# RWKV-5 recurrence and a hierarchical mixture of experts: three items computed in blocks of 32 tokens, small items first, a ring of four weight buffers

## The chip, the cores and the metric

The kernel runs on one core of one Trainium2 chip. The metric is device time in microseconds; of a kernel's runs the median counts. A core has TensorE (PE in the profile; PEld is its weight load), VectorE (DVE), ScalarE (ACT), GpSimd (POOL) and SyncE (SP). SP only issues DMAs here. The profile is of one execution, with times from the start of its span.

## The reference

Two blocks follow each other. The first is a linear recurrence over 768 steps for 4 batches of 8 heads of width 48. Its output is read as 3072 tokens of width 384. The second sends each token to one of 4 groups and to one of 4 experts of that group, and runs that expert alone:

```python
for t in range(S):
    cur = np.einsum('bhd,bhe->bhde', u[None] * kt, vt)
    y[:, :, t] = np.einsum('bhd,bhde->bhe', rt, state + cur)
    state = w[None, :, :, None] * state + np.einsum('bhd,bhe->bhde', kt, vt)
...
for g in range(G):
    ...
    for e in range(Eg):
        mask_e = e_idx == e
        h = np.maximum(xg[mask_e] @ w1[g, e], 0.0)
        ye = h @ w2[g, e]
        combined = g_w[mask_g][mask_e] * e_w[mask_e]
        out[tok_idx] = combined[:, None] * ye
```

All is FP32. w1 of an expert is 384 x 1024, w2 is 1024 x 384, 3.15 MB together, and there are 16 experts.

## The kernel before

**First stage, up to about 137 us.** The recurrence is computed in chunks of 128 steps. While it runs, tokens are routed and their rows (384 values, a token number and a gate, in four quarters of 98 values) are scattered by POOL to `x_sorted` in HBM, to a region for each expert. When most tokens are routed, the two experts with the most tokens so far are chosen. Their weights are fetched early (`early[0]`, `early[1]`, two pairs of buffers), and their first 128 tokens each are computed ahead (`up_ahead`, `down_ahead`, L1042 to L1061).

Of this stage only one group of instructions matters later: `gate_parts` (L646) writes four matmuls with 32 output rows each to the partition quarters 0, 32, 64 and 96 of one PSUM tile. The array has 128 columns, and each of these uses a group of 32.

**Second stage: the items.** The 16 experts are then worked off as items. `order` (L1073) is the list of slots 1, 2, ..., 15, 0. `SLOTS` gives the number of tokens that a slot computes. Slots 0 and 1 are what is left of the two early experts (96 and 88 tokens), slots 2 to 15 are the other experts, the largest first (212 down to 164). An item at place p has these steps:

- `fetch_rows(p)` (L1093): SP fetches its tokens' rows into `xg`, four DMAs, one for each quarter. Rows have 392 bytes. For the slots 0 and 1 a fifth DMA (L1110) fetches token numbers and gates.
- `fetch_weights(p)` (L1112): SP fetches w1 and w2 in eight DMAs of 384 KB each (L136, L142).
- `columns(p)` (L1119): DVE turns the rows into columns, `xe` (L1123), and makes the list of output rows.
- `arrange(p)` (L1135): ACT copies w2 into another order, `w2p`, in three copies (L1141).
- `up` (L1143), four calls for an item: TensorE multiplies w1, the stationary side, with `xe`, whose columns are tokens. ACT applies Relu into `hT`.
- `down` (L1158), three calls: TensorE multiplies `w2p`, stationary, with `hT`; ACT copies the result to `yT`.
- `finish(p)` (L1168): DVE turns `yT` back (L1172), multiplies by the gates (L1173), and POOL scatters each block of 32 tokens to the output (L1175).

Slots 0 and 1 go another way down: `rows_down` (L239) and `half_down` (L253) have `hT` stationary and w2 streaming in 384 or 2 x 192 columns, ACT scales by the gate (L245, L260), and POOL scatters whole or half rows (L246, L261).

There are three pairs of weight buffers in turn, `turns` (early[1] and two more), and early[0] is kept until the last item. SP works in program order. Its order is: three pieces of weights of p=1, rows 0, rows 1, the other pieces, rows 2, weights 2, and then in item p the rows of p+2 (from p=1 on) and the weights of p+3. Written out: weights 1 (with rows 0 and 1 among them), rows 2, weights 2, weights 3, rows 3, weights 4, rows 4, weights 5 and so on. The DMAs of SP signal over eight semaphores in turn; one is issued when the DMA that had its semaphore last has landed.

Of the kernel before, what the change touches and what calls it, by code (L numbers as in the profile page):

```python
# [21 lines left out]
SLOTS = [96, 88, 212, 208, 208, 202, 202, 200, 200, 196, 194, 188, 186, 174, 172, 164]  # L22
# [7 lines left out]
def kernel(  # L30
# [36 lines left out]
    assert len(SLOTS) == GE and max(SLOTS) <= 256 and sorted(SLOTS[2:], reverse=True) == SLOTS[2:]  # L67

# [50 lines left out]
    tagA = [cst([P, 2], f"tagA_{i}") for i in range(4)]  # L119
    idA = [cst([P, 1], f"idA_{i}", I32) for i in range(4)]  # L120
    idH = [cst([P, 1], f"idH_{z}", I32) for z in range(2)]
    okA = [cst([P, 1], f"okA_{i}", I32) for i in range(4)]
# [130 lines left out]
    def half_down(hT, w2, i, n, z, po, yt):  # L253
        cols = slice(DM // 2 * z, DM // 2 * (z + 1))
        for fo in range(FO):
            nc.tensor.matmul(
                po[0:n, 0 : DM // 2], lhsT=hT[:, fo, 0:n], rhs=w2[:, fo, cols], start=(fo == 0), stop=(fo == FO - 1),
                skip_group_check=True,
            )
        nc.scalar.mul(yt[0:n], po[0:n, 0 : DM // 2], tagA[i][0:n, 1:2])  # L260
        ins = nc.gpsimd.indirect_dma_start(  # L261
            out=out.rearrange("n (z w) -> (n z) w", z=2),
            out_offset=bass.IndirectOffsetOnAxis(ap=idH[z][0:n].bitcast(U32), axis=0),
            in_=yt[0:n], in_offset=None, bounds_check=2 * N - 1, oob_is_err=False,
        )
        tc.declare_no_dep(ins.ins, group="rows out", reason="no piece comes twice")
        tc.add_to_no_dep_group("rows out", ins.ins)

    def tokens(i, n, count, halves=False):
        tag = tagA[i][0:n, 0:1].bitcast(I32)  # L270
        nc.vector.tensor_scalar(out=okA[i][0:n], in0=prow[0:n], scalar1=count[0:n], scalar2=None, op0=OP.is_lt)
        if halves:
            for z in range(2):
                nc.vector.memset(idH[z][0:n], NOWHERE)
            nc.vector.tensor_scalar(out=tag, in0=tag, scalar1=1, scalar2=None, op0=OP.logical_shift_right)
            nc.vector.copy_predicated(idH[0][0:n], okA[i][0:n], tag)
            nc.vector.tensor_scalar(out=tag, in0=tag, scalar1=1, scalar2=None, op0=OP.bitwise_or)
            nc.vector.copy_predicated(idH[1][0:n], okA[i][0:n], tag)
            return
# [783 lines left out]
    with ExitStack() as moe:  # L1063
# [9 lines left out]
        order = list(range(1, GE)) + [0]  # L1073
        last = GE - 1
        turns = [early[1]] + [
# [7 lines left out]
        def held(p):  # L1083
            return early[0] if p == last else turns[p % 3]
# [8 lines left out]
        def fetch_rows(p):  # L1093
# [15 lines left out]
            if s < 2:  # L1109
                nc.sync.dma_start(out=tagA[2 + s][0 : SLOTS[s]], in_=mine[0 : SLOTS[s], Q_ID : Q_ID + 2])  # L1110

# [7 lines left out]
        def columns(p):  # L1119
# [4 lines left out]
            if s < 2:  # L1124
                tokens(2 + s, SLOTS[s], cnt_s[:, s : s + 1], p == last)
                return
# [41 lines left out]
        def finish(p):  # L1168
# [5 lines left out]
            for i in range(nb):  # L1174
                ins = nc.gpsimd.indirect_dma_start(  # L1175
                    out=out_q, out_offset=bass.IndirectOffsetOnAxis(ap=idn[:, i : i + 1].bitcast(U32), axis=0),
                    in_=yt[:, i], in_offset=None, bounds_check=N * NQ - 1, oob_is_err=False,
                )
                tc.declare_no_dep(ins.ins, group="rows out", reason="no piece comes twice")
                tc.add_to_no_dep_group("rows out", ins.ins)  # L1180

        fetch_weights(1, range(3))
        fetch_rows(0)
        fetch_rows(1)
        fetch_weights(1, range(3, NPIECE))
        fetch_rows(2)
        fetch_weights(2)
        columns(0)
# [302 lines left out]
```

## Time and profile before

| | |
|---|---|
| median of 14 runs | 420.35 us (413.02 to 423.34) |
| profiled execution | 414.87 us |
| its span | 413.1 us |
| mean granted TensorE clock | 0.983 |
| item p=0 (slot 1) begins | 161.03 us |
| item p=15 (slot 0) begins | 394.32 us |
| its first and second down half begin | 399.65 and 402.25 us |
| last scatter on POOL | 407.44 us, 0.92 us long |

The profile's page gives the busy time of each engine, then the same in slices, then groups of instructions. The timeline gives instructions in order of time, equal ones merged: start, length from the first to the end of the last, engine, line, operation, tiles, shape, count, and in brackets the idle time before and what ended it. The list of waits gives who waited for what, in total, how often, and the longest. The bracket of a wait names what came last by the profile, and can be off where that had long been done. Ends of matmuls are modelled, their starts are recorded.

The weights' last set of pieces is issued between 354.1 and 363.2 us. The rows' DMA on SP (L1105) is issued, for p=2, at 164.89 us, for p=3 at 189.43, for p=4 at 205.63.

### The profile page before, as it was taken

The page shows a single profiled execution, that of the slowest core. Times are in us where ns is not written, and L with a number is a line of the kernel's source. Part 1 is how long each engine was busy: PE and PEld are TensorE (multiplying, and loading weights), DVE is VectorE, ACT ScalarE, POOL GpSimd, SP SyncE. Part 2 cuts the span into 40 slices and gives each one's busy share as a digit, 9 for nine tenths or more (in the row PEclk, how much of TensorE's full clock was granted, in tenths as well). Part 3 has the DMA queues.
Part 4 walks back from the last instruction along what each step waited for, and adds up shares of the span by engine and source line. Part 5 has one row for each costly group of instructions (what it writes and reads, how often), then busy time and mean ns, then how long its engine had stood idle before and what let it go on. Part 6 is the DMA issues. An engine that isn't in the chain of part 4 may idle for free.

```text
span 413.1 us, 10511 instructions
## 1 busy us (share of the span) xinstructions
PE 395.3 (96%) x3989; PEld 367.5 (89%) x3989; DVE 154.1 (37%) x408; ACT 180.0 (44%) x429; POOL 202.5 (49%) x266
## 2 busy tenths in 40 slices
PE   8999999999879899999999999999999999998992
PEld 6788998888768777799999999999999999998991
DVE  7888988878638431101112112021221221121110
ACT  4666888888545211414424324144143244243210
POOL 7999979987410242001461441623624523532542
PEclk9999999999969899999999999999999999999998
DMA  9999999978939256999999999899989889891000
GB/s 135 177 173 187 213 203 208 223 153 199 297 87 263 87 175 166 274 263 250 238 255 264 212 229 278 208 246 263 214 237 272 217 235 272 197 243 35 27 21 23
DMA packets 121198, 81.80 MB, mean 198 GB/s; under 512 B 94902, under 2 KB 112370, under 8 KB 121141
## 3 DMA queue, kind: packets, MB, share of 16 engines
q1 hardware_dynamic: 114083, 71.12, 75.1%
q0 software_dynamic: 4768, 9.55, 8.0%
q10 hardware_dynamic: 2290, 0.40, 0.7%
q8 instruction: 33, 0.54, 0.6%
q14 instruction: 24, 0.20, 0.2%
HBM read 69.89 MB, written 11.67 MB: 197 GB/s over the span
## 4 chain that ended last, share of the span: by engine, by line
issue 45%; PE 32%; POOL 18%; DVE 2%; another core or an unknown queue 1%; POOLq 1%; ACT 0%; DVEq 0%
POOL out_dram L1175 16%; PE PA L564 6%; PE YB L611 6%; PE TR L545 3%; PE YB L602 2%; PE RW L545 2%; PE TR L646 2%; PE YB L660 2%; PE MS L622 2%; PE MS L674 1%; DVE am L571 1%; PE RW L660 1%; PE PA L459 1%; POOL out_dram L246 1%
## 5 line engine op out<-in xcount | busy, mean ns | idle before, releaser
L1175 POOL DMA_INDIRECT out_dram<-yt,idn x93 | 90.6, 974 | 139.9 <-DVE yt L1173 109.5
L1123 DVE STREAM_TRANSPOSE xe<-xg 128x672 f32<-128x672 f32 (+2 forms) x16 | 12.8, 797 | 131.5 <-DMA xg<-x_sorted 104.2
L1163 PE MATMUL YB<-hT,w2p 128*128 128x208 f32 (+10 forms) x336 | 59.2, 328 | 1.2 <-issue 1.2
L1163 PE MATMUL PA<-hT,w2p 128*128 128x208 f32 (+10 forms) x336 | 58.8, 327 | 0.2 <-ACT yT L1166 0.2
L1163 PEld LDWEIGHTS YB<-hT,w2p 128*128 128x128 f32 x336 | 55.7, 190 | 1.7 <-issue 1.7
L1163 PEld LDWEIGHTS PA<-hT,w2p 128*128 128x128 f32 x336 | 55.1, 190 | 1.4 <-ACT yT L1166 0.8
L589 ACT ACTIVATE am<-ident,du 128x128 f32<-128x128 f32 x152 | 50.6, 399 | 0.0
L1141 ACT COPY w2p<-w 128x1024 f32<-128x1024 f32 x42 | 41.1, 1046 | 4.4 <-DMA w<-in_moe_w_dram 4.4
L1172 DVE STREAM_TRANSPOSE yt<-yT 128x672 f32<-128x672 f32 (+1 forms) x14 | 11.8, 843 | 72.5 <-ACT yT L1166 72.5
L571 DVE COPY_PREDICATED am<-later,PA 128x1024 f32<-128x1024 int32 x24 | 32.6, 1357 | 11.7 <-PE PA L564 9.4
L1151 PE MATMUL RW<-xe,w 128*128 128x208 f32 (+12 forms) x192 | 32.8, 320 | 0.0
L1151 PE MATMUL TR<-xe,w 128*128 128x208 f32 (+12 forms) x192 | 32.8, 320 | 0.0
L1151 PE MATMUL MS<-xe,w 128*128 128x208 f32 (+12 forms) x192 | 32.8, 320 | 0.0
L1151 PE MATMUL SB<-xe,w 128*128 128x208 f32 (+12 forms) x192 | 32.7, 320 | 0.0
L1151 PEld LDWEIGHTS SB<-xe,w 128*128 128x128 f32 x192 | 30.8, 190 | 0.6 <-issue 0.2
L1151 PEld LDWEIGHTS MS<-xe,w 128*128 128x128 f32 x192 | 30.7, 190 | 0.0
L1151 PEld LDWEIGHTS RW<-xe,w 128*128 128x128 f32 x192 | 30.7, 190 | 0.0
L1151 PEld LDWEIGHTS TR<-xe,w 128*128 128x128 f32 x192 | 30.7, 190 | 0.0
L231 POOL DMA_INDIRECT x_sorted<-xt,place_i x16 | 16.1, 1006 | 26.4 <-DMA w<-in_moe_w_dram 17.4
L564 PE MATMUL PA<-rT,kT 48*64 48x64 f32 (+1 forms) x768 | 27.9, 264 | 0.1
L611 PE MATMUL YB<-am,vt 128*48 128x128 f32 x384 | 27.1, 283 | 0.7 <-DVE am L571 0.6
L564 PEld LDWEIGHTS PA<-rT,kT 48*64 48x64 f32 x768 | 21.9, 139 | 5.0 <-issue 4.3
(229 smaller groups left out, 570.5 us busy)
## 6 DMA issues: line engine op xcount, KB each, us to landing
w<-in_moe_w_dram SPq DMA_DIRECT2D x128, 384.0 KB
vt<-in_v_dram SPq DMA_DIRECT2D x24, 192.0 KB
rp<-in_r_dram SPq DMA_DIRECT2D x23, 192.0 KB
kt<-in_k_dram SPq DMA_DIRECT2D x22, 192.0 KB
xg<-x_sorted SPq DMA_DIRECT2D x36, 85.8 KB
x_sorted<-zeros SPq DMA_DIRECT2D x4, 392.0 KB
out_dram<-yt,idn POOLq DMA_INDIRECT x93
xg<-x_sorted SPq DMA_DIRECT2D x20, 73.5 KB
```

Of the source, the lines that this page charges most:

```text
L231: ins = nc.gpsimd.indirect_dma_start(out=xs_dram, out_offset=bass.IndirectOffsetOnAxis(ap=place_i[:, i : i + 1], axis=0), in_=xt[:, i].rea ...
L545: nc.tensor.transpose(ps[:, hc, :], two, ident)
L564: nc.tensor.matmul(PA[64 * z : 64 * (z + 1), e, P * hc + 64 * z : P * (hc + 1)], lhsT=kT[rows, hc, 64 * z : 64 * (z + 1)], rhs=rT[rows, hc ...
L571: nc.vector.copy_predicated(am[n % NAM], later.unsqueeze(1).unsqueeze(1).to_broadcast([P, 2, HC, P]).bitcast(I32), PA.rearrange("p e (h t) ...
L589: nc.scalar.mul(am[n % NAM][:, e, hc, :], ident, dus[n][:, i : i + 1])
L611: nc.tensor.matmul(y_at(e, hc), lhsT=vt[:, n % 2, 2 * hc + e, :], rhs=amn[:, e, hc, :], start=(n < 4 and hc < 2), stop=True, skip_group_ch ...
L660: nc.tensor.transpose(ps[:, q // 2, P * (q % 2) : P * (q % 2 + 1)], yT[:, q // 2, q % 2, :], ident)
L1123: nc.vector.transpose(xe[:, :, 0:nb, :], xg[:, 0:nb, 0:QW].rearrange("p i (ko a) -> p ko i a", a=32))
L1141: nc.scalar.copy(o4[:, kk], v4[:, kk])
L1151: nc.tensor.matmul(ph[:, i, 0:n], lhsT=w1[:, ko, P * (f + i) : P * (f + i + 1)], rhs=xe[:, ko].rearrange("p i b -> p (i b)")[:, 0:n], star ...
L1163: nc.tensor.matmul(po[:, 0:n], lhsT=w2p[:, d, fo, :], rhs=hT[:, fo, 0:n], start=(fo == 0), stop=(fo == FO - 1))
L1175: ins = nc.gpsimd.indirect_dma_start(out=out_q, out_offset=bass.IndirectOffsetOnAxis(ap=idn[:, i : i + 1].bitcast(U32), axis=0), in_=yt[:, ...
```

## The change

Three items are computed in blocks of 32 tokens: slots 0, 1 and 11. In such a block the tokens are the stationary side (32 columns of the array), and the weights stream, as four matmuls that write to the four partition quarters. Up: for each of the 3 parts of the 384 inputs, four matmuls of 256 columns; ACT applies Relu, DVE turns the result into `hT`. Down: for each of the 8 parts of the 1024 hidden values, four matmuls of 96 columns; DVE scales the result by the gate from PSUM, POOL scatters the block. w2 is used as it lies, so these items have no `arrange`.

The order becomes slots 1, 0, then 2 to 15 without 11, then 11. The weights have one ring of four pairs of buffers, and an item's weights are fetched one item earlier than before (`p + 4`). The rows are fetched at `p + 2` as before. The slots' sizes are rounded up to multiples of 32 where items are by block: 88 to 96 and 188 to 192. `half_down`, the fifth DMA of `fetch_rows` and the half-row lists go.

SP's order becomes: weights 2 (with rows 0 and 1 among them), rows 2, weights 3, weights 4, rows 3, weights 5, rows 4, weights 6 and so on.

```diff
-SLOTS = [96, 88, 212, 208, 208, 202, 202, 200, 200, 196, 194, 188, 186, 174, 172, 164]
+SLOTS = [96, 96, 212, 208, 208, 202, 202, 200, 200, 196, 194, 192, 186, 174, 172, 164]
+
+BY_BLOCK = (0, 1, 11)
...
-        order = list(range(1, GE)) + [0]
+        order = [1, 0] + [s for s in range(2, GE) if s not in BY_BLOCK] + [BY_BLOCK[2]]
         last = GE - 1
-        turns = [early[1]] + [
+        turns = [early[1], early[0]] + [
...
         def held(p):
-            return early[0] if p == last else turns[p % 3]
+            return turns[p % 4]
...
-            if s < 2:
-                nc.sync.dma_start(out=tagA[2 + s][0 : SLOTS[s]], in_=mine[0 : SLOTS[s], Q_ID : Q_ID + 2])
...
+        def up_block(p, i):
+            if i == 0:
+                hTs[p] = pool.tile([P, FO, 256], FP32, tag="hT", name="hT")
+            w1, xe = held(p)[0], xes[p]
+            ph = next_of(ups)[:, 0 : F // NQ]
+            for ko in range(KO):
+                wq = w1[:, ko].rearrange("p (fo q a) -> p q fo a", q=NQ, a=32)
+                for q in range(NQ):
+                    nc.tensor.matmul(
+                        ph[32 * q : 32 * (q + 1)].rearrange("p (fo a) -> p fo a", a=32), lhsT=xe[:, ko, i, :],
+                        rhs=wq[:, q], start=(ko == 0), stop=(ko == KO - 1), skip_group_check=True,
+                    )
+            hq = pool.tile([P, F // NQ], FP32, tag="hq", name="hq")
+            nc.scalar.activation(hq, ph, AF.Relu)
+            nc.vector.transpose(hTs[p][:, :, 32 * i : 32 * (i + 1)], hq.rearrange("p (fo a) -> p fo a", a=32))
+
+        def down_block(p, i, yt):
+            w2, hT, idn, xg = held(p)[1], hTs[p], ids[p], xgs[p]
+            po = next_of(downs)
+            for fo in range(FO):
+                for q in range(NQ):
+                    nc.tensor.matmul(
+                        po[32 * q : 32 * (q + 1), 0:QW], lhsT=hT[:, fo, 32 * i : 32 * (i + 1)],
+                        rhs=w2[:, fo, QW * q : QW * (q + 1)], start=(fo == 0), stop=(fo == FO - 1),
+                        skip_group_check=True,
+                    )
+            nc.vector.tensor_scalar(
+                out=yt[:, i], in0=po[:, 0:QW], scalar1=xg[:, i, Q_GATE : Q_GATE + 1], scalar2=None, op0=OP.mult
+            )
+            block_out(idn, yt, i)
...
-        fetch_weights(1, range(3))
+        fetch_weights(2, range(3))
         fetch_rows(0)
         fetch_rows(1)
-        fetch_weights(1, range(3, NPIECE))
+        fetch_weights(2, range(3, NPIECE))
         fetch_rows(2)
-        fetch_weights(2)
+        fetch_weights(3)
         columns(0)
         for p in range(GE):
+            if by_block(p):
+                for i in range(blocks(p)):
+                    up_block(p, i)
+                    if i == 0 and p > 0 and not by_block(p - 1):
+                        finish(p - 1)
+                if p == 1:
+                    fetch_rows(p + 2)
+                if p < last:
+                    columns(p + 1)
+                yt = pool.tile([P, 8, QW], FP32, tag="yt", name="yt")
+                for i in range(blocks(p)):
+                    down_block(p, i, yt)
+                    if i == 0 and p + 1 < GE and not by_block(p + 1):
+                        arrange(p + 1)
+                if p + 4 < GE:
+                    fetch_weights(p + 4)
+                continue
             up(p, 0)
             up(p, 2)
-            if p > 1:
+            if not by_block(p - 1):
                 finish(p - 1)
-            if 0 < p and p + 2 < GE:
+            if p + 2 < GE:
                 fetch_rows(p + 2)
             up(p, 4)
             up(p, 6)
...
-            if p + 3 < last:
-                fetch_weights(p + 3)
-            if p + 1 < last:
+            if p + 4 < GE:
+                fetch_weights(p + 4)
+            if not by_block(p + 1):
                 arrange(p + 1)
```

## The prediction

> **What bounds the kernel now.** I read the page's busy row first, then the table by stage, then TensorE's timeline, then the queue of SP.
>
> ```profile
> PE 395.3 (96%) x3989; PEld 367.5 (89%) x3989; DVE 154.1 (37%) x408; ACT 180.0 (44%) x429; POOL 202.5 (49%) x266
> 200.00:350.00 150.00, 149.80 (x891) 148.58 (x890) 26.87 (x58) 54.27 (x94) 62.30 (x64) 1.00 0.96 242
> ```
>
> The first line is the whole span, the second one stage (PE, PEld, DVE, ACT, POOL, then granted clock, DMA share, GB/s). In the expert stage TensorE never rests (149.80 of 150 us), but the DMA share is 0.96 too: two things are full at once. The queue of SP tells which one leads:
>
> ```profile
> SPq L1105 <- DMA w<-in_moe_w_dram: 32.8, 33, 1.7
> SPq L136 <- DMA w<-in_moe_w_dram: 31.0, 27, 3.2
> SPq L142 <- PE YB L1163: 0.3, 1, 0.3
> ```
>
> SP issues weights (L136, L142) and rows (L1105), and it waits for earlier transfers to land, 64 us in these two lines, and for TensorE 0.3 us. So the weight stream runs at its own pace, whatever TensorE does. How near it is to TensorE:
>
> ```profile
> 171.52 2.31 PE L1151 MATMUL SB<-xe,w 128*128 128x212 f32 x12
> 188.72 2.27 PE L1151 MATMUL SB<-xe,w 128*128 128x208 f32 x12
> 205.60 2.27 PE L1151 MATMUL SB<-xe,w 128*128 128x208 f32 x12
> ...
> 189.43 5.80 SPq L1105 DMA_DIRECT2D xg<-x_sorted  x4
> ...
> 203.71 0.88 DVE L1123 STREAM_TRANSPOSE xe<-xg 128x672 f32<-128x672 f32 x1 [10.43 <-PE YB L1163]
> 220.01 0.88 DVE L1123 STREAM_TRANSPOSE xe<-xg 128x672 f32<-128x672 f32 x1 [12.07 <-DMA xg<-x_sorted]
> ```
>
> Items p=1, 2, 3 begin on TensorE at 171.52, 188.72 and 205.60. The rows of p=3 were issued at 189.43, behind three sets of weights, and could be transposed only at 203.71: done at 204.6, 1.0 us before TensorE wanted them. (The first transpose's wait is put down to a matmul long done; the rows' last packets ended at 202.4 in the trace, so it is the rows.) Those of p=4 come at 220.01, 16.3 us later.
>
> **A matmul's price.** An FP32 matmul is two instructions here (L1163: 672 for 14 items of 24). Sixteen of 384 columns take 5.17 us (166.35 to 171.52), twelve of 208 take 2.11, of 164 1.67: 0.834 ns a column and 2.5 ns each. Below about 130 columns the 128-wide weight load binds: twelve of 88 or 96 take 1.33 us, 111 ns each. What four column groups of 32 do is shown by the gate matmuls, in two narrow windows of the timeline:
>
> ```profile
> 29.27 0.40 PE L646 MATMUL TR<-yT,gwp 128*32 128x128 f32 x8
> 29.38 0.29 PE L646 MATMUL TR<-yT,gwp 128*32 128x128 f32 x4
> ```
>
> Sixteen began in rounds of four, one round each 0.11 us (29.27, 29.38): a round of four costs what one instruction of 128 columns costs (0.834 x 128 + 2.5 = 109 ns). So the groups run side by side in full. The Trainium skill is less hopeful: "TensorE: Matmul & The Clock Gate", section "Measured speedup vs the span model", has three column tiles at 2.38 times one, 79% of full. By it, as an estimate, a block would take 3.3 us instead of the 2.62 below, and the last item 4 us more. The rounds of the trace decide for 2.62.
>
> **The change, part by part.**
> - Up in a block: 3 ko x 2 = 6 rounds of 256 columns, 216 ns each: 1.30 us. Down: 8 fo x 2 = 16 rounds of 96, 82.5 ns: 1.32. A block: 2.62 us.
> - Slot 1, first: 161.03 to 171.52 = 10.49 us becomes 3 x 2.62 = 7.85. Slot 0, from last to second: 394.32 to 404.85 = 10.5 becomes 7.85. Slot 11, now last: 96 x 159 ns = 15.3 becomes 6 x 2.62 = 15.7. TensorE's sum: -4.9 us.
> - Off the path: one arrange less (3 x 1.05 us of ACT), no tag DMAs (0.35 us each of SP), no token arithmetic (under 1 us of DVE). New on DVE: 12 transposes of 256 columns, 0.45 us by the rows of 288 (0.48) and 384 (0.56), and 12 scalings, between 0.17 (the smallest rows) and 0.76 us (576 columns, L1173); I take 0.25. All lie beside 1.3 us of matmuls; PSUM alternates, so a scaling has a block's time to spare. They queue behind columns(p+1), which waits for rows; for p=1 those of p=2 came at 173.25, and its first down block ends at about 174.
> - The queue of SP. The sequence of transfers keeps its shape: weights, two small fetches of rows, weights, rows, weights, weights, rows, weights, rows. What before was set 1 for p=1 is now set 1 for p=2. So the rows of p=3 still come behind set 3, and set 3 is now that of p=4. The fourth buffer has every set fetched one item earlier, and the rows, which stand behind it in the same queue, are not. **The stream does not get faster, and TensorE now reaches p=3 earlier:** 161.03 + 2 x 7.85 + 17.2 (slot 2) = 193.9, where before it came at 205.60. The rows are there at 203.7, less what the smaller fetch for slot 0 saves (0.2 MB and two tag DMAs, 0 to 1.5 us, I take 1.0), plus 0.9 of transpose: 203.6. TensorE stands for 9.7 us, and the saving of the small items is gone before it counts; up to 9.7 us the first two items could even be dearer for nothing.
> - The clock. After the idle stretches before 116.2 and before 136.4 the trace shows half speed: sixteen L611 take 1.95 us at 120.06 against 1.08, back to normal by 122.8; twelve L826 take 2.93 against 1.50. Half speed lasted 6.6 us (116.2 to 122.8) and 3.5 us (136.4 to 139.9), so 3.3 and 1.7 us were lost. After 9.7 us of rest I take 2.5, ends 0 and 3.3.
> - Items 3 to 13 then go at the pace of before: 175.05 us (205.60 to 380.65), and 1.6 more, since slot 3 (208) stands in them and slot 11 (188) has left: p=14 begins at 203.6 + 2.5 + 176.7 = 382.8. It takes 13.7 as before: p=15 begins at 396.4 (p=15 before: 394.32).
> - The tail. Before, POOL's last scatter ended at 408.36, 14.0 us after p=15 began, and the span 4.8 later. Now POOL has six scatters of p=14 (ready some 4.2 us into p=15, as its copy and 1.6 us of DVE follow the first up block), then six of its own, 1.28 us apart: the last begins at 4.2 + 11 x 1.28 = 18.3 and ends at 19.3. TensorE is done at 15.7, so POOL sets it by about 2 us. End: 396.4 + 19.3 + 4.8 = 420.5 us of span.
>
> The profiled execution took 414.87 us with a span of 413.1 (1.7 around it), so this makes 422.2: +7.4. But the 14 runs have a median of 420.35, 5.5 above the profiled one. If the stream of transfers is a few per cent slower in those, rows set p=14's start in both kernels, the half clock is absorbed, and what is left is the end: p=15 dearer by 19.3 - 14.0 = 5.3. Between 5.3 and 7.4 I take 6.2: **426.5 us**, own range 423.5 to 430.
>
> **Rivals.**
> 1. *The rows come in time, and it is faster.* If the stream was paced by something that the fourth buffer frees, TensorE runs through: p=2 begins at 176.7, slot 2 takes 17.2, and slots 3 to 15 without 11 take 205.6 - 15.3 (188.72 to 394.32 before), so p=15 begins at 384.2, 10.1 earlier than before. With 24.1 us from there to the end instead of 18.8 the sum is -4.8: 415.5. It decides if r3 lands before 194, 8.5 us earlier. Against: 0.3 us of waits for TensorE in SP's queue.
> 2. *Blocks dearer than four side by side.* A down round asks for a matmul every 20.6 ns for 1.3 us on end. By their start times the trace has 16 at 20.9 ns, but its fastest 256 on end at 43 (with waits among them), and the whole first 111 us hold 2035 in 107.56 us of busy TensorE, 53 ns each. At 43, a down block takes 2.75 us: six of them add 8.6 us in the last item (the first two items hide theirs in the stall): 435. Anything over 20.6 counts there. The same page, section "Wait — 56ns, not 53.3ns?", gives some 62 ns a matmul where firmware decodes it. By that, as an estimate, it would be 16 us instead of 8.6; the 53 ns of the first stage are below it already.
> 3. *Nearly nothing.* The half clock is absorbed, rows come at the early end and POOL's queue overlaps more: +1 to +4, some 423.
>
> **Chances.** Main case 0.58 (423.5 to 430), rival 1 0.12, rival 2 0.14, rival 3 0.16. One per cent, about what a measurement of this kernel tells from no change, is 4.2 us, so slower is above 424.6 and faster below 416.1: slower 0.69 (0.55 of the main case, 0.14), same 0.19, faster 0.12. The range leaves out rival 1 and half of rival 2: 417.5 to 432.5.
>
> **What would show it.** Right: no matmul from about 194 to 203; then some microseconds with the clock halved; the third fetch of seven blocks of rows still issued near 189, its transpose near 203; a down block of 1.3 us; POOL scattering without a gap until the end. Wrong: TensorE at p=3 before 198, rows fetched ahead of the third set, or a down block above 1.6 us.

## The result and the profile after

The changed kernel takes 437.82 us (median of 10 runs, 433.36 to 441.96), the kernel before 419.99 (47 runs): a ratio of 1.0512, 95% interval 1.0469 to 1.0556. The forecast was 426.5 us and its range ended at 432.5: the direction was right, the size was not. The profiled execution took 434.19 us with a span of 432.5. (Some executions of a kernel fall into a slower state; the ratios here and below leave them out on both sides, so they are not the ratios of the medians, 1.042 here.)

The page of the changed kernel: TensorE's row of busy time, and the row of the queue that brings instructions (transfers, MB, share of 16 engines):

```profile
PE 401.1 (93%) x4805; PEld 366.1 (85%) x4805; DVE 159.1 (37%) x425; ACT 175.7 (41%) x420; POOL 205.5 (48%) x269
...
q8 instruction: 39, 0.64, 0.6%
```

The table by stages, 200 to 350 us:

```profile
200.00:350.00 150.00, 148.62 (x872) 147.55 (x871) 25.27 (x54) 51.15 (x89) 59.48 (x62) 1.00 0.97 241
```

TensorE has 816 matmuls more than before and is busy for 5.8 us more, but the span has grown by 19.4: the rest is time in which it stands. Little of that lies in the stage of 200 to 350 us (busy for 148.62 us of 150, before 149.80). Most lies in the three items by block. TensorE's timeline, p=0 and p=1 (start, us, engine, line, tiles, shapes, count, idle time before and what ended it):

```profile
158.58 1.50 PE L1169 MATMUL SB<-w,xe 128*32 128x256 f32 x24
...
162.49 1.50 PE L1182 MATMUL PA<-w,hT 128*32 128x96 f32 x64
163.81 1.50 PE L1182 MATMUL YB<-w,hT 128*32 128x96 f32 x64
165.13 0.59 PE L1182 MATMUL PA<-w,hT 128*32 128x96 f32 x10
166.06 1.21 PE L1182 MATMUL PA<-w,hT 128*32 128x96 f32 x44 [0.34 <-issue]
170.47 0.69 PE L1182 MATMUL PA<-w,hT 128*32 128x96 f32 x9 [3.20 <-issue]
170.80 0.65 PE L1169 MATMUL TR<-w,xe 128*32 128x256 f32 x3
...
182.72 0.41 PE L1182 MATMUL YB<-w,hT 128*32 128x96 f32 x6 [0.34 <-issue]
187.25 1.17 PE L1182 MATMUL YB<-w,hT 128*32 128x96 f32 x18 [4.11 <-issue]
188.35 4.61 PE L1127 MATMUL RW<-xe,w 128*128 128x212 f32 x12
```

The two blocks that run undisturbed take exactly what was forecast, 1.32 us a down block (162.49, 163.81, 165.13). In the third block of each item the stream of matmuls breaks off, for 3.2 and 4.1 us, and the word behind the arrow is "issue": as far as the profile shows, no semaphore, no data and no buffer was waited for. Over the whole execution the matmuls of the down blocks (L1182) have this one entry of idle time before them:

```profile
  issue: 13.0, 15
```

(For matmuls and weight loads together, which run beside each other, it says 29.7 us and counts most stops twice.) From the first matmul of p=0 to the first of p=2 TensorE stands 8.8 of 29.8 us. It also works slower there than forecast: the mean granted clock is 0.85, and the passes behind a stop take up to twice their time.

TensorE's timeline in the last item:

```profile
408.08 1.00 PE L1182 MATMUL YB<-w,hT 128*32 128x96 f32 x16
409.43 0.37 PE L1182 MATMUL YB<-w,hT 128*32 128x96 f32 x4 [0.35 <-issue]
410.14 0.39 PE L1182 MATMUL YB<-w,hT 128*32 128x96 f32 x6 [0.35 <-issue]
411.58 0.55 PE L1182 MATMUL YB<-w,hT 128*32 128x96 f32 x4 [1.05 <-issue]
...
414.44 1.39 PE L1182 MATMUL YB<-w,hT 128*32 128x96 f32 x27 [0.87 <-issue]
...
415.63 2.68 PE L1182 MATMUL PA<-w,hT 128*32 128x96 f32 x60
```

GpSimd's timeline in the same microseconds:

```profile
408.48 0.97 POOL L1154 DMA_INDIRECT out_dram<-yt,idn  x1 [0.30 <-issue]
409.76 0.97 POOL L1154 DMA_INDIRECT out_dram<-yt,idn  x1 [0.30 <-issue]
411.04 0.97 POOL L1154 DMA_INDIRECT out_dram<-yt,idn  x1 [0.30 <-issue]
412.32 0.97 POOL L1154 DMA_INDIRECT out_dram<-yt,idn  x1 [0.30 <-issue]
```

Here TensorE does not break off once, it limps: a few matmuls, a stop, a few more, and this as long as GpSimd issues the scatters of p=14 one behind the other. The first block takes 7.4 us so. The second is whole but at half clock (granted 0.50): 2.6 us. From the fourth on there is one stop of 0.6 us in each, from one matmul's start to the next one's.

What the forecast was built on, the waits of SP (us in total, times, longest):

```profile
SPq L138 <- DMA w<-in_moe_w_dram: 25.2, 24, 1.9
SPq L1086 <- DMA w<-in_moe_w_dram: 24.8, 23, 1.5
SPq L1086 <- DVE yt L1149: 22.7, 6, 11.7
...
SPq L138 <- PE MS L1127: 4.7, 3, 2.2
```

And the transpose of the rows of p=3 in VectorE's timeline:

```profile
196.95 0.88 DVE L1102 STREAM_TRANSPOSE xe<-xg 128x672 f32<-128x672 f32 x1 [8.18 <-DMA xg<-x_sorted]
```

SP still waits for transfers, hardly for TensorE. (The third row is the wait for a free row buffer; 20.9 of its 22.7 us come after 300 us, when the stream is far ahead.) The rows of p=3 come late, at 197 (forecast 203). But TensorE comes later still. The ledger, from the timeline:

| point of TensorE's timeline | forecast, us | measured, us |
|---|---|---|
| p=0 begins | 161.0 | 158.6 |
| p=2 begins | 176.7 | 188.35 |
| p=3 begins | 203.6 | 207.85 |
| p=15 begins | 396.4 | 400.3 |
| last matmul ends | 412.1 | 425.7 |
| end of the span | 420.5 | 432.5 |

The 12.0 us by which the span was missed are 3.9 until p=15 begins, 9.7 in the last item (25.4 us instead of 15.7), and -1.6 behind it. Of the 14.1 us by which the first two items were missed, most is not in this sum: 7.4 of them fall where the forecast had put its wait at p=3 (p=2 and the wait took 19.5 us instead of 26.9), and 2.4 had been gained before p=0. So the miss of the total is mainly the last item's.

### The profile page after: what moved, and what is told of

Same layout as the page of the kernel before. It is cut to its first block, busy times and chain, and to the rows that moved or that the text cites. A ratio compares the mean times of both kernels' runs of the same rounds, so it can differ in the third digit from the quotient of the medians.

```text
span 432.5 us, 12166 instructions
## 1 busy us (share of the span) xinstructions
PE 401.1 (93%) x4805; PEld 366.1 (85%) x4805; DVE 159.1 (37%) x425; ACT 175.7 (41%) x420; POOL 205.5 (48%) x269
## 5 line engine op out<-in xcount | busy, mean ns | idle before, releaser
L1154 POOL DMA_INDIRECT out_dram<-yt,idn x99 | 96.4, 974 | 169.9 <-DVE yt L1149 106.4
L1139 PE MATMUL YB<-hT,w2p 128*128 128x202 f32 (+9 forms) x304 | 54.3, 329 | 3.3 <-issue 3.2
L1139 PE MATMUL PA<-hT,w2p 128*128 128x208 f32 (+9 forms) x320 | 55.9, 328 | 0.0
L1139 PEld LDWEIGHTS YB<-hT,w2p 128*128 128x128 f32 x304 | 50.2, 190 | 4.7 <-issue 4.7
L1127 PE MATMUL RW<-xe,w 128*128 128x208 f32 (+9 forms) x156 | 30.0, 345 | 0.0
L542 PE MATMUL PA<-rT,kT 48*64 48x128 f32 (+1 forms) x768 | 27.1, 256 | 1.9 <-issue 1.4
L1127 PE MATMUL TR<-xe,w 128*128 128x208 f32 (+9 forms) x156 | 27.7, 328 | 0.0
L1127 PE MATMUL SB<-xe,w 128*128 128x208 f32 (+9 forms) x156 | 27.7, 327 | 0.0
L1127 PE MATMUL MS<-xe,w 128*128 128x208 f32 (+9 forms) x156 | 27.7, 327 | 0.0
L542 PEld LDWEIGHTS PA<-rT,kT 48*64 48x64 f32 x768 | 21.1, 132 | 6.9 <-issue 5.5
L589 PEld LDWEIGHTS YB<-am,vt 128*48 128x48 f32 x384 | 20.7, 125 | 5.6 <-issue 4.2
```

The costliest lines, as they stand in the source:

```text
L542: nc.tensor.matmul(PA[64 * z : 64 * (z + 1), e, P * hc + 64 * z : P * (hc + 1)], lhsT=kT[rows, hc, 64 * z : 64 * (z + 1)], rhs=rT[rows, hc ...
L589: nc.tensor.matmul(y_at(e, hc), lhsT=vt[:, n % 2, 2 * hc + e, :], rhs=amn[:, e, hc, :], start=(n < 4 and hc < 2), stop=True, skip_group_ch ...
L1127: nc.tensor.matmul(ph[:, i, 0:n], lhsT=w1[:, ko, P * (f + i) : P * (f + i + 1)], rhs=xe[:, ko].rearrange("p i b -> p (i b)")[:, 0:n], star ...
L1139: nc.tensor.matmul(po[:, 0:n], lhsT=w2p[:, d, fo, :], rhs=hT[:, fo, 0:n], start=(fo == 0), stop=(fo == FO - 1))
L1154: ins = nc.gpsimd.indirect_dma_start(out=out_q, out_offset=bass.IndirectOffsetOnAxis(ap=idn[:, i : i + 1].bitcast(U32), axis=0), in_=yt[:, ...
```

## The experiments

Theory A: TensorE is not slowed by the matmuls but by the supply of its instructions. Rival B: matmuls of column groups cannot be issued every 20.6 ns for long, or the groups do not run side by side. (The expectations of set 1 call them theory 1 and theory 2.) The kernels were run in five sets, each on one chip. The kernel before took 431.58, 429.9, 398.28, 431.57 and 398.2 us in them, so a time is read against its own set, and mostly the lengths of items inside a profile are read. A single run has no interval of its own.

**Set 1.** `wide` streams every down matmul's columns twice (192 instead of 96), with as many instructions:

```diff
-                        po[32 * q : 32 * (q + 1), 0:QW], lhsT=hT[:, fo, 32 * i : 32 * (i + 1)],
-                        rhs=w2[:, fo, QW * q : QW * (q + 1)], start=(fo == 0), stop=(fo == FO - 1),
+                        po[32 * q : 32 * (q + 1), 0 : 2 * QW].rearrange("p (z w) -> p z w", z=2),
+                        lhsT=hT[:, fo, 32 * i : 32 * (i + 1)],
+                        rhs=spread(w2[:, fo, QW * q : QW * (q + 1)], 1, 2), start=(fo == 0), stop=(fo == FO - 1),
```

> The changed kernel, but every matmul of a down block streams its 96 columns twice, so a round asks for 165 ns of streaming instead of 82.5, with the same number of instructions; the output is the same. Theory 1 (instructions reach TensorE too slowly: beyond a store of some 340 instructions a matmul with its weight load costs about 47 ns, 25.4 us for the 528 of the last item): the streaming of the last item, 6 x (1.30 + 2.62) = 23.5 us, still fits under that, so the last item stays at 25 to 27 us and the span within 432 to 437. Theory 2 (the down matmuls themselves are dearer than four side by side, 2.93 us a block): twice the columns make a down block 5 to 6 us, the last item 38 to 43 us, the span above 445.

448.71 us (one run). TensorE's timeline, the down blocks of p=0:

```profile
163.25 2.78 PE L1182 MATMUL PA<-w,hT 128*32 128x192 f32 x64
165.85 2.78 PE L1182 MATMUL YB<-w,hT 128*32 128x192 f32 x64
168.45 2.78 PE L1182 MATMUL PA<-w,hT 128*32 128x192 f32 x63
```

A block takes 2.60 us, twice 1.30, without a stop. Yet p=0 and p=1 together, from the first matmul of p=0 to the first of p=2, take 29.4 us, against 29.8 in the changed kernel. Doubling the work of the array cost these two items nothing. That speaks for A. The last item does get longer, 30.4 us: neither the 25 to 27 expected under A nor the 38 to 43 under B. Five of its six blocks run undisturbed, at 2.6 us each. The span, 447.0, is on B's side (above 445), but it was expected from the first profile, and here the kernel before is slower too.

`half` leaves out every second contraction step of the down blocks, and with it half of their instructions:

```diff
-            for fo in range(FO):
+            for fo in range(0, FO, 2):
...
```

> The changed kernel, but the down blocks leave out every second of the 8 parts of the hidden values, so 32 matmuls a block instead of 64. Theory 1: the last item has 336 matmuls with their loads instead of 528; at 47 ns beyond the store that is between 11.8 us (streaming alone, 6 x 1.96) and 15.8; the two small items 168 each, 6 to 8 us, hardly a stall in them. TensorE then reaches the fourth item early and waits there for its rows, until about 200 us. Theory 2: a down block costs half of 2.93, the last item 7.8 + 8.8 = 16.6 us, in even steps without long stalls.

442.82 us (one run). Now p=0 and p=1 take 15.3 us, with no stop for instructions over 0.5 us, and at once the wait that the forecast had put there appears: TensorE stands 8.2 us at p=3 for its rows, until 204.40 (forecast: 203.6). It had been hidden behind the late instructions. The last item limps as before, from 421.2 to 426.8, and takes 21.3 us, not the 11.8 to 15.8 expected under A. Its six stops of 0.5 to 1.3 us come to 5.2 us, in the changed kernel to 5.0: with half of the instructions the limp is as long.

`pairs` computes the down part for 64 tokens at a time in two column groups of 64: a quarter of the instructions, each twice as wide, and a scatter of half rows. (The third block of a small item goes down as before.)

```diff
+            for fo in range(FO):
+                for z in range(2):
+                    nc.tensor.matmul(
+                        po[64 * z : 64 * (z + 1), 0:HW], lhsT=hT[:, fo, 64 * j : 64 * (j + 1)],
+                        rhs=w2[:, fo, HW * z : HW * (z + 1)], start=(fo == 0), stop=(fo == FO - 1),
...
```

> The changed kernel, but two blocks of 32 tokens go down together: 64 tokens stationary, two column groups of 64, 192 columns streaming, half rows scattered. The streaming time is the same (2.62 us for two blocks), the instructions are a quarter: 32 matmuls for 64 tokens instead of 128. Theory 1: the last item has 240 matmuls and takes 15.7 us, the small ones 168 each and 8 us each; the issue stalls are gone, TensorE comes to the fourth item at about 193 and waits for rows until 200 to 203; the span is then what was forecast without the issue limit, 415 to 421, some 1 to 2% slower than before. Theory 2 (column groups do not run side by side in accumulating matmuls): the last item stays near 25 us and the time near 437.

437.02 us (4 runs), 1.0115 of the kernel before (1.0043 to 1.0188). The two items take 18.0 us with stops of 0.5 us at most, the last item 17.7 (expected 16 and 15.7). And the wait for rows at p=3 is there, with the half clock behind it (4.53 us for twelve matmuls of 208 columns instead of 2.27):

```profile
192.95 3.03 PE L1157 MATMUL PA<-hT,w2p 128*128 128x212 f32 x16
202.03 4.53 PE L1145 MATMUL RW<-xe,w 128*128 128x208 f32 x12 [6.04 <-DVE xe L1106]
```

`small_only` leaves slot 11 whole and in its place, and slot 15 last:

```diff
-BY_BLOCK = (0, 1, 11)
+BY_BLOCK = (0, 1)
...
-        order = [1, 0] + [s for s in range(2, GE) if s not in BY_BLOCK] + [BY_BLOCK[2]]
+        order = [1, 0] + list(range(2, GE))
...
```

> Slots 0 and 1 first and by block, ring of four; slot 11 whole and in its place, slot 15 last and whole, so that its turn back and six scatters come after the last matmul. Theory 1: the first two items take about 30 us together as in the changed kernel (their instructions are the same), then no issue stall; the last item of 13.7 us is followed by about 14 us instead of 7; span some 428 to 432. A theory that the last item alone is to blame would have the first two items at 16 to 18 us here.

441.81 us (one run). The loss of the first two items is whole without the last one: 29.3 us. The last item runs without stops (13.5 us), but its copies and scatters lie bare behind it, 12.4 us from the last matmul to the end against 6.8. (The spans expected of `pairs`, 415 to 421, and of `small_only`, 428 to 432, were missed at 435.6 and 440.0; they too came from the first profile.)

**Where the stops are.** Counted from the trace, TensorE's stops of over 1 us in p=0 and p=1, from one instruction's start to the next one's, come at these numbers of its instructions (matmuls, weight loads and semaphores counted from the start of the program, in kernels with the same sequence of instructions up to there):

```
changed kernel   5569: 3.44 us                 6081: 4.36 us
wide                            5825: 2.20 us  6081: 3.58 us
small_only       5569: 2.70 us  5825: 3.66 us  6081: 4.29 us
```

The numbers are 256 apart, wherever in the work of a block they fall, and a transfer on the instruction queue has 16 KB, 256 instructions of 64 bytes. In the changed kernel these transfers run from 167.71 to 169.07 and from 184.29 to 185.63, and TensorE goes on at 170.47 and 187.25, 1.4 and 1.6 us behind their ends. From entering a piece to the start of the transfer of the next one it takes 4.2 to 6.2 us in these two items. A piece of 256 holds 127 matmuls or so, 2.6 us of work at the forecast pace. In the whole items a piece lasts some 20 us (transfers start at 210.35, 234.14, 253.51, 274.96), so such a delay is hidden there. The Trainium skill says of this, in "Runtime: NRT & Kernel Launch", section "Instruction fetch mechanics", that instructions come in blocks of 16 KiB, that the next block is fetched while the current one runs, and that the fetch is mostly hidden. The traces agree on the blocks; here the fetch is not hidden.

The limp of the last item is something else. Between 408.3 and 414.5 us no transfer of instructions or weights runs; the only queue with packets is that of the scatters:

```profile
q0 software_dynamic: 160, 0.20, 10.7%
```

So A, late pieces, is the account for p=0 and p=1 alone.

**Set 2.** `quiet` asks for the weight sets 2 to 5 only behind p=1, in a ring shifted by two:

```diff
-            return turns[p % 4]
+            return turns[p] if p < 2 else turns[(p - 2) % 4]
...
-        fetch_weights(2, range(3))
...
-        fetch_weights(2, range(3, NPIECE))
...
-        fetch_weights(3)
...
+                if p == 1:
+                    for nxt in (2, 3, 4, 5):
+                        fetch_weights(nxt)
+                    arrange(2)
```

> The weights of sets 2 to 5 are asked for only after item p=1, so that the DMA queues have little to carry while TensorE runs p=0 and p=1 by block; item 2 then has to wait for its weights, and the whole is slower than the changed kernel by 15 to 40 us, which is the price of the setting and no evidence. Read are the lengths of p=0 and p=1. Theory A (TensorE's instructions come in pieces of 256, and a piece that is asked for while the weight stream fills the DMA queues lands only some 7 us after it is asked for; with empty queues in 1 to 2 us): p=0 and p=1 together 16 to 20 us instead of 29.8, and no stop of over 0.7 us at instructions 256 apart. Rival B (matmuls of four column groups cannot be issued faster than one in about 47 ns for long, whatever else runs): 27 to 30 us, as before.

451.4 us (one run). The table by stretches of `quiet` (PE, PEld, DVE, ACT, POOL, clock, DMA share, GB/s), p=0's down blocks and p=1's:

```profile
164.00:168.50 4.50, 4.12 (x194) 3.81 (x186) 1.64 (x7) 0.38 (x1) 1.30 (x2) 1.00 0.05 15
...
172.50:176.50 4.00, 4.00 (x170) 3.70 (x160) 2.23 (x8) 0.38 (x1) 0.89 (x1) 1.00 0.86 183
```

The same table of the changed kernel, p=0's down blocks:

```profile
163.00:171.00 8.00, 4.46 (x180) 3.93 (x175) 1.64 (x7) 0.12 (x1) 1.94 (x2) 0.87 1.08 243
```

With a DMA share of 0.05 the next piece's transfer starts 0.6 us after a piece is entered, there is no stop at a piece's end, and p=0 takes 8.7 us (forecast 7.85, changed kernel 12.2). As soon as p=0's buffer is free, SP's queue fills it, the DMA share goes to 0.86 and 1.03 within p=1, the delay grows to 3.2 us and there is a stop of 1.2 us at a piece's end; p=1 takes 12.4. Together, to the end of p=1's last matmul, 21.1 us, 1 over what A expected and 6 under B: the instructions wait behind the weights. The setting was quiet for p=0 only. (The whole was 5 us slower than the changed kernel in this set, not the 15 to 40 expected of the setting.)

`late_finish` puts the scatters of p=14 behind the last item's down blocks:

```diff
-                    if i == 0 and p > 0 and not by_block(p - 1):
+                    if i == 0 and 0 < p < last and not by_block(p - 1):
...
+                if p == last:
+                    finish(p - 1)
```

> The six scatters of item p=14 stand behind the last item's down blocks instead of beside its up blocks. Theory A2 (the halting start of the last item's down phase, eight stops of 0.5 to 1.3 us between 408.8 and 414.4 in the changed kernel, is the time in which GpSimd issues these six scatters one behind the other; they hold up the instruction supply of TensorE, and of ScalarE too): the stops are gone, the last item from its first to its last matmul takes 16 to 20 us instead of 25.4, single stops of 0.6 us at its own scatters stay; the end comes 11 to 15 us after the last matmul instead of 6.8, so the time moves by -4 to +3 us. Rival B (the matmuls themselves cannot be issued faster than one in 47 ns): the item stays at 24 to 26 us and the time rises by 6 to 8 us.

445.86 us (one run), 19.5 us from the last item's first matmul to its last. TensorE's timeline:

```profile
419.12 1.50 PE L1182 MATMUL YB<-w,hT 128*32 128x96 f32 x64
420.44 1.50 PE L1182 MATMUL PA<-w,hT 128*32 128x96 f32 x64
421.76 1.50 PE L1182 MATMUL YB<-w,hT 128*32 128x96 f32 x64
423.08 0.64 PE L1182 MATMUL PA<-w,hT 128*32 128x96 f32 x12
424.06 0.39 PE L1182 MATMUL PA<-w,hT 128*32 128x96 f32 x6 [0.34 <-issue]
```

The limping start is gone: 204 matmuls in 4.3 us, 21 ns each, with the weight stream over and no row of scatters beside. B falls: the array and the issue of column groups can keep the forecast pace, at least for three blocks. From the fourth block on there are five such stops of 0.6 us (0.34 to 0.38 by the brackets, which count from the end of the matmul before), beside the item's own scatters. The whole down phase takes 11.7 us against 17.7. The time did not fall (the changed kernel in this set: 446.4), as the span ends 13.3 us after the last matmul.

`again` is the changed kernel itself:

> The changed kernel itself, on the chip of these runs, as their measure. All theories: 1.045 to 1.058 of the kernel before; p=0 and p=1 together 28 to 31 us, the last item 24 to 27 us.

446.4 us (4 runs), 1.049 (1.0321 to 1.066), 28.9 us for the two items with stops at 5569, 5825 and 6081 (2.50, 3.38, 4.13 us), 25.6 for the last.

`pairs_rows` is `pairs` with every item's rows asked for one item earlier:

```diff
-            xg = xgs[p] = pool.tile([P, 8, QX], FP32, tag="xg", bufs=3, name="xg")
+            xg = xgs[p] = pool.tile([P, 8, QX], FP32, tag="xg", bufs=4, name="xg")
...
         fetch_rows(2)
+        fetch_rows(3)
         fetch_weights(3)
...
-            if p + 2 < GE:
-                fetch_rows(p + 2)
+            if p + 3 < GE:
+                fetch_rows(p + 3)
```

> As pairs (down blocks of 64 tokens in two column groups), and every item's gathered rows are asked for one item earlier, ahead of the weight set they stood behind, with four row buffers. Theory (once the instruction supply no longer delays TensorE, item p=3 waits for its rows, 6.0 us in pairs, and only because they are queued behind weight set 3): no wait for rows at p=3, 5 to 8 us less than pairs, 0.985 to 1.002 of the kernel before. Rival (the weight stream itself is late, rows or not): the wait moves to the weights of p=3 or p=4, at most 2 us are gained, 1.005 to 1.02.

424.74 us (11 runs), 0.9939 (0.9877 to 1.0). There is no wait at p=3. As forecast, it was the place of the rows in the queue.

**Set 3.** `order_only` keeps the order and the ring of four, and computes all items whole:

> The order and the ring of four alone: both small items first and whole (10.5 us each as before), slot 11 whole in its place, slot 15 last with its scatters behind it; no item by block. By the steps of the prediction: TensorE reaches p=3 at about 196 us and waits for its rows until about 203.5, some 5 to 8 us, 2 us more at half clock, and the tail of a large item costs 4 us more than that of a small one: 1.02 to 1.035 of the kernel before. Rival (rows in time, the order costs nothing but its tail): 1.005 to 1.015, no wait for rows at p=3.

412.11 us (4 runs), 1.0312 (1.0267 to 1.0358). TensorE's timeline before p=3:

```profile
184.36 3.03 PE L1146 MATMUL PA<-hT,w2p 128*128 128x212 f32 x16
195.41 4.53 PE L1134 MATMUL SB<-xe,w 128*128 128x208 f32 x12 [8.03 <-DVE xe L1106]
```

`order_rows` adds the rows one item earlier to it:

> As order_only, with every item's rows asked for one item earlier and four row buffers. Theory (the wait at p=3 is the place of the rows in the queue): no wait at p=3, 6 to 10 us less than order_only, 1.00 to 1.015 of the kernel before. Rival (the weight stream is late): within 2 us of order_only.

404.46 us (4 runs), 1.0127 (1.0085 to 1.0169), no wait at p=3. The rows' place costs 7.7 us where TensorE is in time for them. The rest, 6.2 us, is the tail of a large item: 12.3 us from the last matmul to the end in both, against 6.4 in a profile of the kernel before from such a chip (`before_look`, below).

`after_rows` is the changed kernel with the rows one item earlier:

> The changed kernel with the rows one item earlier and four row buffers, and nothing else. Theory (the late instruction supply has eaten the wait for rows, TensorE reaches p=3 only when they are there): within 2 us of the changed kernel, 1.042 to 1.056 of the kernel before. Rival (the rows still cost the changed kernel something, at p=3 or later): 5 us or more are gained, under 1.04.

405.99 us (4 runs), 1.0165 (1.0121 to 1.0208). By the number it is the rival's side, but the changed kernel was not in this set, and the profile differs from the earlier ones in more than the rows. On this chip the last item does not limp although p=14's scatters run beside it. TensorE's timeline:

```profile
388.56 1.50 PE L1182 MATMUL YB<-w,hT 128*32 128x96 f32 x64
389.88 1.50 PE L1182 MATMUL PA<-w,hT 128*32 128x96 f32 x64
391.20 1.50 PE L1182 MATMUL YB<-w,hT 128*32 128x96 f32 x64
392.52 1.85 PE L1182 MATMUL PA<-w,hT 128*32 128x96 f32 x64
```

The last item takes 17.1 us. The stops at 5569 and 6081 are there as on the other chips (3.33 and 4.69 us), and the two items take 25.8.

`rows_late` is `pairs_rows` with an item's scatters beside the next item's later down passes, and five row buffers:

> As pairs_rows, and the scatters of an item are issued beside the next item's second and third down pass instead of beside its up passes (five row buffers). Theory (a row of scatters on GpSimd holds up ScalarE and TensorE, as in the last item: in pairs_rows the last relu of item 3 starts 4.2 us after its matmuls end, at 208.25, while scatters run, and TensorE stands 2.6 us for it; some items show it, others not): the stops of 1 to 3 us in the middle of items are gone, 5 to 20 us less than pairs_rows, 0.95 to 0.985 of the kernel before. Rival (the stops have another cause, or the scatters hold up the copies of the down passes just as well): 0.985 to 1.01.

401.38 us (12 runs), 1.0043 (1.0008 to 1.0078), by the number the rival's side. It could not be decided: no profile of this set shows a stop in the middle of items, so there was none to take away. The scatters, now later, draw out the end to 10.7 us after the last matmul.

**Set 4.** The changed kernel, its form with early rows, and `pairs_rows`, side by side:

> The changed kernel once more, with its rows-early form beside it on one chip. The kernel before took 420, 431.6, 429.9 and 398.3 us in the four sets of runs so far, and where it took 398.3 no profile shows a stop of TensorE beside scatters. Theory (the loss has two parts: the late instruction pieces in p=0 and p=1, on every chip, and the halts beside scatters in the last item, only on chips that show them): where the kernel before takes under 405 us, 1.02 to 1.034 of it, p=0 and p=1 together 25 to 28 us and the last item 16.5 to 19 us; where it takes over 418 us, 1.043 to 1.058 and 24 to 27 us for the last item. Rival (the ratio is the kernel's own): 1.045 to 1.057 on any chip.

> The changed kernel with the rows one item earlier, beside again2. Theory: where the kernel before takes under 405 us, 1 to 5 us less than again2 (there TensorE reaches p=3 some 2 us before its rows); where it takes over 418 us, within 2 us of again2. Rival (the rows early are what made 1.0165 of 1.05): 10 us or more less than again2 on any chip.

> pairs_rows again, for an interval of its own and beside the changed kernel: 0.985 to 0.999 of the kernel before by the theory (each small item 1.5 to 2.4 us shorter than before, the end 3 us later than with a small item last, and slot 11 at 15 to 17 us); 1.00 to 1.01 if the gain seen so far was this chip's halts falling otherwise.

442.92 us (4 runs), 1.0267 (1.0194 to 1.0339); 441.48 (4), 1.0262 (1.0201 to 1.0323); 427.02 (6), 0.9865 (0.98 to 0.9931). The two items of `again2` take 29.5 us, its last one 25.7, as in the first profile, and the rows earlier change nothing that can be told: they are masked. But the ratio is smaller than 1.043, so my expectation failed here, and that of the rival too: the changed kernel loses the same in its items by block. That the kernel before loses more elsewhere on this chip would explain it; it was not profiled there. In all profiles of sets 1, 2 and 4 TensorE stops in the middle of whole items as well: the intervals of over 0.42 us from one matmul's start to the next, between 215 us and the last item, come to 12 to 19 us (`quiet` left out, which waits there for weights); in the profile of 432.5 us it was 4.5.

**Set 5** was to show this in the kernel before. `before_look` is that kernel, `one_scatter` and `after_one` issue one scatter per whole item:

```diff
-            for i in range(nb):
+            for i in range(1):
```

> The kernel before itself, for a profile on this chip. Theory (on some chips rows of scatters hold up TensorE and ScalarE in the middle of items, and that is why the kernel before takes 398 on one chip and 430 on another): where it takes over 425 us, 10 to 25 us of stops of over 0.42 us between 215 us and the last item, in several items, where the profile of 413.1 us had 2.0; where it takes under 405 us, under 1 us. Rival (those chips are slower in something else): stops under 4 us at over 425 us too.

> The kernel before with only the first block's scatter of each large item; the other blocks' rows of those items are left out of the output. Theory: the stops in the middle of items are gone, and where the kernel before takes over 425 us this one takes 10 us less or more than 10; where it takes under 405 us, within 3 us of it, apart from the end, which has no scatters of the last large item to wait for in either. Rival (the stops have nothing to do with scatters): the same stops and the same time within 4 us.

> The changed kernel with only the first block's scatter of each item that is computed whole; the other blocks' rows of those items are left out of the output, the scatters of the items by block stay. Theory: no halting start of the last item's down phase (the item 16.5 to 20 us); the stops at pieces of 256 instructions in p=0 and p=1 stay (25 to 30 us for the two); 8 to 14 us above one_scatter, which is what the change costs without the halts beside rows of scatters. Rival (the halting start belongs to the dense matmuls): the last item 24 to 26 us, 17 us or more above one_scatter.

The chip of this set was again one without such stops: 398.67 (8 runs), 399.27 (8) and 414.39 us (2), 1.0014 (0.9996 to 1.0032), 1.0017 (0.9999 to 1.0034) and 1.0401 (1.0371 to 1.0431). So the first two decide nothing about the scatters. The page of `before_look`, its first row, shows how full TensorE is there:

```profile
PE 385.0 (97%) x3989; PEld 361.7 (91%) x3989; DVE 153.3 (39%) x408; ACT 180.4 (46%) x429; POOL 202.1 (51%) x266
```

`after_one` came to 15.1 us above `one_scatter`, 1 more than expected. The two items take 29.2 us with stops at 5569, 5825 and 6081 (3.14, 1.80, 6.33 us), the last item 17.9, and it ends 10.5 us after its last matmul. So the change loses without any limp too. (With one scatter for a whole item there is no row of them beside the last item, so this run does not tell whether the chip would show the limp.) How much is not settled: `after_rows` took 8.4 us less on another chip of this kind, 3.4 of them in the two items, 0.9 in the last item and 4.0 behind it, none in a wait at p=3, which neither has.

## Why the prediction was wrong

**A matmul's price.** Right for the array. Six rounds of 256 columns took 1.30 us and sixteen of 96 took 1.32; `wide` doubled the second to 2.60. Four groups run side by side in full, and the factor of 2.38 for three, from the Trainium skill's "TensorE: Matmul & The Clock Gate", section "Measured speedup vs the span model", is not seen in these rows of FP32 with four groups.

**The failing step: that an item is the sum of its blocks,** 3 x 2.62 = 7.85, 7.85 and 6 x 2.62 = 15.7 us. They took 12.2, 17.5 and 25.4. The price per matmul was that of the array, and the supply of instructions was put at nothing. In p=0 and p=1 instructions come in pieces of 256, the next one asked for when a piece is entered, and what ends last is their arrival, held up behind the weight stream (the stops 256 apart and `wide` show the first, `quiet`, one run, the second): 14.1 us more than forecast in the first profile, and 8 to 14 in the others with the same instructions (24.1 to 29.5 us in `after_rows2` to `again2`), on every chip. The last item took 9.7 us more: some 6 in the limp of its first block, 1.3 at half clock behind it, most of the rest in three stops of 0.6 us. That the scatters of p=14 bring the limp is shown by `late_finish` (moved, and the limp is gone; the item still takes 3.8 us more than forecast). They do not bring it everywhere: in `after_rows`, on another chip, the same scatters ran beside the item and there was none. What holds TensorE in the limp stays open; it is not a late piece, and it is as long with half of the instructions (`half`).

**The sign** was right, but in the changed kernel not by the forecast's path: the wait at p=3, its largest term, did not occur there.

**Rival 2** had the sign and nearly the time, 435, from the question how long a matmul every 20.6 ns can go on. Its bound of 43 ns was not the mechanism: with instructions at hand 204 matmuls take 21 ns each. And it held that the first two items hide their extra cost in the wait for rows; they needed more than that wait was worth.

**The weight stream's own pace and the rows behind set 3.** Right, and masked. TensorE would have stood 6.0 to 8.2 us at p=3 (`pairs`, `half`, `order_only`; forecast 9.7), and stands there no more when the rows are asked for earlier. In the changed kernel it came to p=3 only at 207.85, by when they were there. `order_only` shows the forecast's wait at work without any items by block: 1.0312.

**The half clock.** Right in size, in another place: up passes after a stop took 2.2 to 2.9 us longer (`half`, `pairs`, `order_only`; forecast 2.5). In the changed kernel it follows the stops for instructions, at p=1 and p=2.

**Items 3 to 14** took 192.4 us, forecast 192.8. The agreement is luck in part: the forecast holds 2.5 us of half clock at p=3, which did not come, and the items themselves took 2 us longer. **The tail** was to be set by GpSimd, 8.4 us behind the last matmul; TensorE was so late that it came 6.8 behind it.

**The version without the dense instructions** (`pairs_rows`) was faster than the kernel before in set 4, 0.9865, and at the edge of it in set 2, 0.9939; it was not run on a chip where the kernel before takes 398 us. Its form with later scatters (`rows_late`) was, and took 1.0043 there.

## What to carry to other kernels

Price a matmul in a second coin, its instructions: four for every FP32 matmul of the program (32 of them in a down block give 64 matmul records, each with a weight load), 256 to a transfer, and with the DMA queues full of weights 7.4 to 9.2 us from one transfer to the next in p=0 and p=1 of the first profile. Splitting a matmul into column groups keeps the array's time and multiplies the instructions, so compare its pace with that supply, as `wide` and `pairs` did, by doubling the columns or taking away instructions. A wait that disappears from the profile after a change may only be hidden behind a newer one: the rows of p=3 were late all along.

## What the runs showed of the hardware

- Instructions compete with data. Entering a piece, the next one's transfer started after 0.6 us at a DMA share under 0.1 (`quiet`, p=0), and after 1.2 to 6.7 us in p=0 and p=1 with the weights under way; the transfer took 0.9 to 1.4 us, and at the stops 1.3 to 1.8 more passed before TensorE went on.
- Beside rows of scatters on GpSimd (0.97 us each, one every 1.28), TensorE at 20 ns per matmul got 1 to 6 matmuls between stops of 0.5 to 1.3 us, on some chips, while no instructions were being fetched. ScalarE was late there too: the relu of the last item's sixth block started at 413.02, its matmuls having been followed by others from 408.08. On the chips where the kernel before takes 398 us neither was seen. What differs between the chips stays open, and so does how much of the kernel before's 398 to 432 us it is: it was profiled only at 413.1 and at 395.6 us of span, where its stops of this kind came to 2.0 and 0 us. Of the 17.5 us between these two profiles 12.8 are there before p=0 begins (161.03 and 148.19 us): from 100 to 148 us TensorE is busy for 42.20 us in the slower one, for 47.96 in the other.
